# Cosformer attention and a token mixer on one core: two heads stacked per row tile, single-copy q, column tiles, 256 KB stores and a written-out order

## The chip, the cores and the metric

The kernel runs on one core of one Trainium2 chip. The metric is the device time of that core in microseconds (us), as the median of several executions. The profile comes from one execution and counts from the first to the last instruction; that is its span.

A core has five engines that each work through a queue of their own in order: PE (TensorE, matmuls, with weight loads listed as PEld), DVE (VectorE), ACT (ScalarE), POOL (GpSimd) and SP (SyncE, which here only issues DMAs). They wait for each other by semaphores. TensorE writes to PSUM, from which VectorE and ScalarE read.

## What is computed

B = 8, 8 heads, S = 576 tokens, D = 64 per head, all inputs and the output in fp32.

```python
# attention, per batch and head
r_q, r_k = relu(q), relu(k)                       # 576 x 64
q_p = concat([r_q * cos, r_q * sin], -1)          # cos, sin of pi/2 * position / 576
k_p = concat([r_k * cos, r_k * sin], -1)          # 576 x 128
kv  = k_p.T @ v                                   # 128 x 64
z   = k_p.sum(0)
x   = (q_p @ kv) / (q_p @ z + 1e-6)               # 576 x 64; heads side by side: 576 x 512
# token mixer, per batch
wq, wk = x @ w_q, x @ w_k                         # 576 x 64
mixed  = (wq @ wk.T / 8) @ x                      # as wq @ (wk.T @ x): 64 x 512 between
out    = relu(mixed) @ w_out                      # 576 x 512
```

## The kernel before

The input of one pair of heads lies in HBM as 128 partitions (two heads by 64 rows) by 9 x 64 numbers: partition p of a head holds the nine consecutive tokens 9p to 9p + 8, called chunks c below. H counts blocks of two such pairs (four heads), 16 in all; g counts pairs, 32 in all; b counts batches, and a batch has two blocks. All matmuls are in bf16.

For one block, `load` (L73) brings k, q and v in three DMAs of 576 KB (the first block's in halves). ScalarE makes relu of k (`relu_k`, L164). POOL makes relu of q, written twice side by side (`dup_q`, L197: 2304 numbers a partition), and casts v (`cast_v`, L184). VectorE multiplies k by cos and sin (`mul_k`, L173: 2304 numbers).

For one pair, `qk_pe` (L201) issues 18 matmuls of K'V (L209: 64 rows, 128 features, 65 columns: v and a column of ones for z) and 18 transposes of q (L216), all into one PSUM tile `qk_ps`. VectorE copies K'V out (L221) and multiplies the transposed q by cos and sin (L223; the upper 64 partitions hold cos, the lower ones sin). `num` (L228) issues, for each of two heads, five matmuls of 128 rows and one that adds the 1e-6 (L236, L239). VectorE takes the reciprocal of the denominators (L241) and multiplies (L242); the result is x, in bf16.

The mixer follows one batch behind: `xT` transposes x (L252; ten 128x128 transposes for a block); `wk_stage` (L268, 20 matmuls), `wq_stage` (L282, eight of 288 columns; w_q stands twice so that both row halves hold the result), `kx_stage` (L293, five of 512 columns), `mx` (L309, four steps of two 64-row matmuls), and `wout` (L327), four matmuls of 512 columns for each row tile of 128 tokens, 36 row tiles in all. Each of these results goes through one of two PSUM buffers of two banks (`m2_tile`, L63), and nearly all are copied out by ScalarE (`copy`, L260; relu of mixed, L316). In the last stages VectorE takes some (L262, L318). Tokens stay in the order of the chunks, so a row tile is stored by two DMAs of 64 rows, 128 KB each, whose rows lie nine tokens apart in the output (L341).

Every engine runs its instructions in the order in which the program text issues them. That order is set by the loop over g (L368 to L406) and a tail written out behind it (L408 to L422). SP's queue holds loads and stores in one line: `load(H + 3)` stands at the head of block H's loop body, the stores where `wout` is called. Fourteen warm-up matmuls (L92) and the constants come first.

Of the kernel before, what the change touches and what calls it, by code (L numbers as in the profile page):

```python
# [15 lines left out]
I32 = mybir.dt.int32  # L17
AF = mybir.ActivationFunctionType
ALU = mybir.AluOpType
FMAX = 3.4028234e38  # L20
EPS_HI = 9.9837780e-07


@with_exitstack
def kernel(
# [15 lines left out]
    P = 128  # L41
    NPAIR = NH // 2
    C9 = (2 * S) // P
    NDM = DM // P
    SC = S // P + 1
    scale_moe = 1.0 / math.sqrt(DH)

    NB = 2 * B
    HC = C9 * D
    SLOTS = C9 + 1  # L50

    consts = ctx.enter_context(tc.tile_pool(name="consts", bufs=1))
    inp = ctx.enter_context(tc.tile_pool(name="inp", bufs=4))
    prep = ctx.enter_context(tc.tile_pool(name="prep", bufs=2))
    small = ctx.enter_context(tc.tile_pool(name="small", bufs=3))
    xpool = ctx.enter_context(tc.tile_pool(name="xpool", bufs=3))
    moe = ctx.enter_context(tc.tile_pool(name="moe", bufs=2))
    mixpool = ctx.enter_context(tc.tile_pool(name="mixpool", bufs=2))
    outpool = ctx.enter_context(tc.tile_pool(name="outpool", bufs=3))
    psum = ctx.enter_context(tc.tile_pool(name="psum", bufs=1, space=bass.MemoryType.PSUM))  # L60
    ctx.enter_context(tc.manual_schedule())

    def m2_tile(dtype, name):  # L63
        return psum.tile([P, 2, 512 if dtype is FP32 else 1024], dtype,
                         name=name, tag="m2", bufs=2)

    srcs = {}
    for nm, src in (("k", k), ("q", q), ("v", v)):
        srcs[nm] = [src[b].flatten().rearrange("(pr p e) -> p pr e", pr=NPAIR, p=P)
                    for b in range(B)]  # L70
    raw = {}

    def load(H, nsplit=1, names=("k", "q", "v")):  # L73
        b, h0 = divmod(2 * H, NPAIR)
        step = 2 // nsplit
        for nm in names:
            raw[nm, H] = inp.tile([P, 2, HC], FP32, name=f"{nm}f")
        for sp in range(nsplit):
            for nm in names:
                lo = sp * step  # L80
                nc.sync.dma_start(raw[nm, H][:, lo:lo + step, :],
                                  srcs[nm][b][:, h0 + lo:h0 + lo + step, :])

    load(0, nsplit=2)

    warm = consts.tile([P, 512], BF16)
    nc.vector.memset(warm, 1.0)
    warm_ps = m2_tile(FP32, "warm_ps")

    def warm_up(n):  # L90
        for _ in range(n):
            nc.tensor.matmul(warm_ps[:, 0, :], warm[:, 0:P], warm,  # L92
                             start=True, stop=True)

    warm_up(14)

    wq_f = consts.tile([P, NDM, DH], FP32)
    wk_f = consts.tile([P, NDM, DH], FP32)
    wo_f = consts.tile([P, NDM, DM], FP32)

    coef = math.pi / 2.0 / S
    ki = consts.tile([P, C9, 2], I32)
    qi = consts.tile([P, C9, D], I32)
    for hh in range(2):
        ph = slice(64 * hh, 64 * hh + 64)
        nc.gpsimd.iota(ki[ph, :, 0], pattern=[[-1, C9]], base=S, channel_multiplier=-C9)
        nc.gpsimd.iota(ki[ph, :, 1], pattern=[[1, C9]], base=0, channel_multiplier=C9)
    nc.gpsimd.iota(qi[0:64], pattern=[[-1, C9], [-C9, D]], base=S, channel_multiplier=0)
    nc.gpsimd.iota(qi[64:128], pattern=[[1, C9], [C9, D]], base=0, channel_multiplier=0)
    cossin = consts.tile([P, C9, 2, D], BF16)  # L110
    cst = consts.tile([P, C9, D], BF16)
    nc.scalar.activation(cossin, ki.unsqueeze(3).to_broadcast([P, C9, 2, D]),
                         AF.Sin, bias=0.0, scale=coef)
    nc.scalar.activation(cst, qi, AF.Sin, bias=0.0, scale=coef)

    ident = consts.tile([P, P], BF16)
    make_identity(nc, ident)

    ones_t = consts.tile([P, P], BF16)
    nc.gpsimd.memset(ones_t, 1.0)  # L120
    eps_t = consts.tile([P, SC], BF16)
    nc.gpsimd.memset(eps_t, 0.0)
    nc.gpsimd.memset(eps_t[0:1, :], EPS_HI)
    nc.gpsimd.memset(eps_t[32:33, :], 1.0e-6 - EPS_HI)

    v_bufs, qpt_bufs, xT_bufs = [], [], []
    for i in range(3):
        vb = consts.tile([P, 2, C9, D + 2], BF16, name=f"v_buf{i}")
        nc.gpsimd.memset(vb[:, :, :, D:D + 2], 1.0)
        v_bufs.append(vb)  # L130
    for i in range(3):
        qb = consts.tile([P, 2, SLOTS, D], BF16, name=f"qpt_buf{i}")
        nc.gpsimd.memset(qb[:, :, 0, :], 0.0)
        qpt_bufs.append(qb)
    for i in range(2):
        xb = consts.tile([P, NDM, SLOTS * D], BF16, name=f"xT_buf{i}")
        nc.gpsimd.memset(xb[:, :, 0:D], 0.0)
        xT_bufs.append(xb)

    wqq_sb = consts.tile([P, NDM, 2, DH], BF16)  # L140
    wk_sb = consts.tile([P, NDM, DH], BF16)
    wo_sb = consts.tile([P, NDM, DM], BF16)

    def load_w():
        nc.sync.dma_start(wq_f, moe_w_q.rearrange("(c p) j -> p c j", p=P))
        nc.sync.dma_start(wk_f, moe_w_k.rearrange("(c p) j -> p c j", p=P))
        nc.sync.dma_start(wo_f, moe_w_out.rearrange("(c p) n -> p c n", p=P))

    def cast_w(part):
        if part == 0:  # L150
            nc.scalar.copy(wqq_sb, wq_f.unsqueeze(2).to_broadcast([P, NDM, 2, DH]))
            nc.scalar.copy(wk_sb, wk_f)
        else:
            nc.scalar.copy(wo_sb[:, 2 * part - 2:2 * part, :],
                           wo_f[:, 2 * part - 2:2 * part, :])

    kp, qd, rks = {}, {}, {}

    def relu_k(H, lo, hi, eng):
        if lo == 0:  # L160
            rks[H] = prep.tile([P, 2, C9, D], BF16, name="rk")
        o = rks[H][:, lo:hi].rearrange("p r c d -> p r (c d)")
        if eng is nc.scalar:
            nc.scalar.activation(o, raw["k", H][:, lo:hi, :], AF.Relu)  # L164
        else:
            eng.tensor_scalar(o, raw["k", H][:, lo:hi, :], FMAX, 0.0,
                              op0=ALU.min, op1=ALU.max)

    def mul_k(H, lo, hi):
        if lo == 0:  # L170
            kp[H] = prep.tile([P, 2, C9, 2, D], BF16, name="kp")
        n = hi - lo
        nc.vector.tensor_mul(  # L173
            kp[H][:, lo:hi],
            rks[H][:, lo:hi].unsqueeze(3).to_broadcast([P, n, C9, 2, D]),
            cossin.unsqueeze(1).to_broadcast([P, n, C9, 2, D]))

    def cast_v(H, lo, hi, eng):
        src = raw["v", H][:, lo:hi, :].rearrange("p r (c d) -> p r c d", c=C9)
        dst = v_bufs[H % 3][:, lo:hi, :, 0:D]  # L180
        if eng is nc.scalar:
            nc.scalar.copy(dst, src)
        else:
            eng.tensor_scalar(dst, src, 1.0, 1.0, op0=ALU.mult, op1=ALU.mult)  # L184

    def dup_q(H, lo, hi, eng):
        if lo == 0:
            qd[H] = prep.tile([P, 2, C9, 2, D], BF16, name="qd")
        n = hi - lo
        dst = qd[H][:, lo:hi].rearrange("p r c w d -> p (r c) w d")  # L190
        src = raw["q", H][:, lo:hi, :].rearrange(
            "p r (c d) -> p (r c) d", c=C9).unsqueeze(2).to_broadcast(
                [P, n * C9, 2, D])
        if eng is nc.scalar:
            nc.scalar.activation(dst, src, AF.Relu)
        else:
            eng.tensor_scalar(dst, src, FMAX, 0.0, op0=ALU.min, op1=ALU.max)  # L197

    xs, kvs, xTs, wkjs, wqTs, kxs, mixs = {}, {}, {}, {}, {}, {}, {}

    def qk_pe(g):  # L201
        H, i = divmod(g, 2)
        qk_ps = psum.tile([P, 2, 2048], mybir.dt.uint8, name="qk_ps", bufs=1)
        qt = qk_ps[:, :, 0:2 * HC].bitcast(BF16)
        kvp = qk_ps[:, :, 2 * HC:2 * HC + 4 * (D + 1)].bitcast(FP32)
        for c in range(C9):
            for hh in range(2):
                p0 = hh * 64
                nc.tensor.matmul(  # L209
                    kvp[:, hh, :], kp[H][p0:p0 + 64, i, c, :, :],  # L210
                    v_bufs[H % 3][p0:p0 + 64, i, c, 0:D + 1],
                    start=(c == 0), stop=(c == C9 - 1))
        for c in range(C9):
            for hh in range(2):
                p0 = hh * 64
                nc.tensor.transpose(  # L216
                    qt[:, hh, c * D:(c + 1) * D],
                    qd[H][p0:p0 + 64, i, c, :, :],
                    ident[p0:p0 + 64, p0:p0 + 64])
# [148 lines left out]
    for g in range(NG):  # L368
# [12 lines left out]
        if g >= 1:  # L381
            num(g - 1)
# [70 lines left out]
```

## Time and profile before

| | us |
|---|---|
| median of 3 runs | 152.29 |
| lowest and highest run | 151.88, 154.79 |
| span of the profiled execution | 149.6 |
| median less that span | 2.7 |
| TensorE busy, of the span | 115.7 |
| VectorE busy | 90.6 |
| ScalarE busy | 88.1 |
| POOL busy | 56.8 |

The execution that was profiled has no time of its own beside its span; the 2.7 us is the distance to the median. The DMAs moved 39.07 MB for the kernel (29.62 MB read, 9.44 MB written, by the page's own account of HBM). The mean granted clock of TensorE is 0.93 of full speed.

To read the page: matmuls overlap, and each record has a pipeline's length of about 0.19 us on it, so the cost of a matmul in a stream is the distance between starts, not its duration. A group's line ends with the idle time of the engine before those instructions and what ended it. In the answer by windows a row has the stretch, its length, the busy time of PE, PEld, DVE, ACT and POOL with counts, the granted clock, the DMA engines' busy share (slightly over 1 is possible) and GB/s.

### The profile page before, as it was taken

What the parts mean: (1) busy time and instruction counts of PE and PEld (TensorE: products, weight loads), DVE (VectorE), ACT (ScalarE), POOL (GpSimd) and SP (SyncE); (2) the same over time, 40 slices, a digit from 0 to 9 for tenths busy, and PEclk for the clock granted to TensorE, in tenths of its full rate; (3) what the DMA queues carried; (4) which work ended last, traced back from release to release, by engine and by line L of the source; (5) the groups of instructions that cost most, each with busy time, mean ns of one, the idle gap of its engine ahead of it and who ended that gap; (6) DMA issues with size and microseconds to landing.
All of it is one profiled execution on the core that took longest, in us unless ns stands there. A gap on an engine that the chain in (4) does not pass through costs nothing. (4 is left out here: it accounts for less than half of the span.)

```text
span 149.6 us, 4978 instructions
## 1 busy us (share of the span) xinstructions
PE 115.7 (77%) x2155; PEld 77.5 (52%) x2182; DVE 90.6 (61%) x156; ACT 88.1 (59%) x114; POOL 56.8 (38%) x56
## 2 busy tenths in 40 slices
PE   6924663969889988998898987888989896894910
PEld 2214553856567657654765665557656664461400
DVE  1278363979777685947596957375959563325110
ACT  8230076467977787668768757687784566243220
POOL 7638248683561808160817164408170000000000
PEclk9985576589999999999999999999999999999996
DMA  5999999999988999996999998999921811566195
GB/s 163 307 397 338 390 391 391 391 390 390 391 279 182 332 302 323 328 379 148 296 326 343 318 400 278 314 296 307 329 81 42 184 31 24 116 143 142 24 203 124
DMA packets 20469, 39.38 MB, mean 263 GB/s; under 512 B 3040, under 2 KB 3040, under 8 KB 20448
## 3 DMA queue, kind: packets, MB, share of 16 engines
q1 hardware_dynamic: 20448, 39.07, 81.2%
q8 instruction: 17, 0.28, 0.7%
q14 instruction: 4, 0.03, 0.1%
HBM read 29.62 MB, written 9.44 MB: 261 GB/s over the span
## 5 line engine op out<-in xcount | busy, mean ns | idle before, releaser
L197 POOL TENSOR_SCALAR qd<-qf 128x2304 bf16<-128x2304 f32 (+1 forms) x17 | 35.6, 2092 | 52.1 <-PE qk_ps L216 30.6
L327 PE MATMUL o_ps<-wo_sb,mix_sb 128*128 128x512 bf16 x124 | 33.6, 379 | 3.6 <-ACT mix_sb L316 1.8
L164 ACT ACTIVATE rk<-kf 128x1152 bf16<-128x1152 f32 (+1 forms) x17 | 18.9, 1111 | 18.4 <-DMA kf<-in_k_dram 9.2
L260 ACT COPY o_sb<-o_ps 128x512 f32<-128x512 f32 (+1 forms) x24 | 18.4, 765 | 17.9 <-PE o_ps L327 8.3
L242 DVE TENSOR_TENSOR x_sb<-num_ps,rec 128x640 bf16<-128x640 f32 x32 | 26.4, 825 | 1.1
L221 DVE CAST kv_sb<-qk_ps 128x130 bf16<-128x130 f32 x32 | 9.4, 293 | 26.7 <-PE qk_ps L216 26.4
L209 PE MATMUL qk_ps<-v_buf,kp 64*128 64x65 bf16 x576 | 15.8, 199 | 11.0 <-POOL v_buf L184 7.2
L223 DVE TENSOR_TENSOR qpt_buf<-qk_ps,cst 128x1152 bf16<-128x1152 bf16 x32 | 23.9, 748 | 0.0
L173 DVE TENSOR_TENSOR kp<-rk,cossin 128x2304 bf16<-128x2304 bf16 (+1 forms) x17 | 22.2, 1305 | 1.6 <-ACT rk L164 1.6
L327 PEld LDWEIGHTS <-mix_sb 128*128 128x128 bf16 x144 | 13.3, 97 | 15.2 <-issue 3.1
L209 PEld LDWEIGHTS <-kp 64*128 64x128 bf16 x576 | 11.9, 99 | 17.2 <-issue 8.7
L316 ACT ACTIVATE mix_sb<-mx_ps 128x576 bf16<-128x576 f32 x29 | 17.5, 655 | 4.7 <-PE mx_ps L309 4.7
L260 ACT COPY xT_buf<-xT_ps 128x1152 bf16<-128x1152 bf16 x15 | 16.8, 1119 | 4.8 <-PE xT_ps L252 4.8
L184 POOL TENSOR_SCALAR v_buf<-vf 128x1152 bf16<-128x1152 f32 x15 | 17.3, 1151 | 1.2
L236 PE MATMUL num_ps<-kv_sb,qpt_buf 128*128 128x65 bf16 x320 | 17.4, 202 | 0.0
L236 PEld LDWEIGHTS <-qpt_buf 128*128 128x128 bf16 x320 | 13.4, 102 | 3.6 <-issue 1.7
L216 PE MATMUL qk_ps<-ident,qd 64*128 64x64 bf16 x576 | 14.8, 197 | 0.0
L309 PE MATMUL mx_ps<-wqT,kx 64*128 64x288 bf16 x64 | 8.0, 285 | 7.0 <-ACT xT_buf L260 3.9
L252 PE MATMUL xT_ps<-ident,x_sb 128*128 128x128 bf16 x160 | 12.2, 227 | 0.2 <-ACT mix_sb L316 0.2
L216 PEld LDWEIGHTS <-qd 64*128 64x128 bf16 x576 | 11.8, 100 | 0.0
L252 PEld LDWEIGHTS <-x_sb 128*128 128x128 bf16 x160 | 10.4, 102 | 1.9 <-issue 0.2
L239 PE MATMUL num_ps<-eps_t,ones_t 128*128 128x5 bf16 x64 | 11.2, 174 | 0.0
(44 smaller groups left out, 97.9 us busy)
## 6 DMA issues: line engine op xcount, KB each, us to landing
out_dram<-o_sb SPq DMA_DIRECT2D x72, 128.0 KB, 3.3
kf<-in_k_dram SPq DMA_DIRECT2D x15, 576.0 KB, 6.7
qf<-in_q_dram SPq DMA_DIRECT2D x15, 576.0 KB, 7.7
vf<-in_v_dram SPq DMA_DIRECT2D x15, 576.0 KB, 8.5
wo_f<-in_moe_w_out_dram SPq DMA_DIRECT2D x1, 1024.0 KB, 9.9
kf<-in_k_dram SPq DMA_DIRECT2D x2, 288.0 KB, 4.0
qf<-in_q_dram SPq DMA_DIRECT2D x2, 288.0 KB, 4.3
vf<-in_v_dram SPq DMA_DIRECT2D x2, 288.0 KB, 5.3
```

The source lines that it names most:

```text
L164: nc.scalar.activation(o, raw["k", H][:, lo:hi, :], AF.Relu)
L173: nc.vector.tensor_mul(kp[H][:, lo:hi], rks[H][:, lo:hi].unsqueeze(3).to_broadcast([P, n, C9, 2, D]), cossin.unsqueeze(1).to_broadcast([P, ...
L197: eng.tensor_scalar(dst, src, FMAX, 0.0, op0=ALU.min, op1=ALU.max)
L209: nc.tensor.matmul(kvp[:, hh, :], kp[H][p0:p0 + 64, i, c, :, :], v_bufs[H % 3][p0:p0 + 64, i, c, 0:D + 1], start=(c == 0), stop=(c == C9 - 1))
L216: nc.tensor.transpose(qt[:, hh, c * D:(c + 1) * D], qd[H][p0:p0 + 64, i, c, :, :], ident[p0:p0 + 64, p0:p0 + 64])
L223: nc.vector.tensor_mul(qpt_bufs[g % 3][:, :, 1:SLOTS, :], qt.rearrange("f h (c d) -> f h c d", c=C9), cst.unsqueeze(1).to_broadcast([P, 2, ...
L236: nc.tensor.matmul(nv[:, hh, u, :], qpt_bufs[g % 3][:, hh, 2 * u:2 * u + 2, :], kvs[g][:, hh, :], start=(u == 0), stop=False)
L242: nc.vector.tensor_tensor(xs[b][:, :, 2 * pr:2 * pr + 2, :].rearrange("p u h d -> p h u d"), nv[:, :, :, 0:D], rec.to_broadcast([P, 2, SC, ...
L252: nc.tensor.transpose(xT_ps[:, i, u * P:(u + 1) * P], xs[b][:, u, 2 * hp:2 * hp + 2, :], ident)
L260: nc.scalar.copy(dst, src)
L316: nc.scalar.activation(dst, mx_ps[:, :, 0:hs], AF.Relu, scale=scale_moe)
L327: nc.tensor.matmul(o_ps[:, r, :], mixs[bp][:, dmc, rt * P:(rt + 1) * P], wo_sb[:, dmc, :], start=(dmc == 0), stop=(dmc == NDM - 1))
```

## The change

The whole body is rewritten. What it does, part by part:

- **K'V.** cos and sin are multiplied into v and no longer into k. VectorE's product (VS) writes v cos and v sin side by side with two more columns each that hold cos and sin themselves, so that z comes out of the same matmul. The stationary operand is relu of k, 64 rows by 64 columns, and the moving one has 130 columns. The four combinations of head pair and row half are four 64x64 tiles of the array, 36 matmuls for a block.
- **q.** POOL writes relu of q once, two heads of different pairs side by side, so a transpose gives 128 features of two heads: 18 transposes for a block. VectorE (QM) writes q cos and q sin of a block in one product of 2304 numbers from PSUM.
- **num.** cos and sin parts are separate matmuls of 64 rows that add up in PSUM: 20 and two small ones for a pair (N).
- **x transposes.** 20 of 64 rows and 64 columns in place of ten of 128 (XT); the copy takes 1280 numbers a partition.
- **wq.** w_q stands once; eight matmuls of 128 rows write to partitions 0 to 63 and 64 to 127 in turn, for two halves of the tokens (WQ). The copy (288 numbers, before 576) puts tokens into their natural order.
- **Stores.** Because of that order a row tile is 128 consecutive rows of the output: one store of 256 KB, 36 in all, from eight buffers.
- **Engines.** relu of k goes from ScalarE to POOL; all of v's casts are on POOL; the weights are cast in six pieces.
- **PSUM.** One two-bank tile for K'V and transposed q (PQ), one for num (PN), two for all else (PM0 and PM1), the latter given out bank by bank where one bank is enough. k, q and v in fp32 have four buffers, their bf16 forms two.
- **Order.** The warm-up matmuls are gone. A text names every step with its number, its bank and its engine, and a loop issues them in that order.

The first and last lines of the order, and the core of the new functions (L stands for a load, ST for a store, E or a swapped name for a copy out of PSUM):

```python
ORDER = """
LV0 LK0 TB0 CV0@G LQ0 LV1 RK0@G VS0@V LK1 RQ0@G KV0 QT0 KE0@V CV1@G RK1@G QM0@V LV2 LQ1 VS1@V N0
...
KX1:11 X9@V KV6 LK8 XT4:0 XK1:11@A XE4:0@A QT6 N10 VS7@V LK9 LQ8 WO2:11 MX6:0 OE2:11@A ME6:0@A
...
ME30:1@A ST26 ST22 WO29:01 ST27 MX28:1 ME28:1@A WO30:00 OE29:01@V WO34:11 WO35:10 ST29 OE30:00@A
ST30 OE34:11@A ST28 ST34 WO33:00 WO32:01 OE35:10@A ST35 OE33:00@A ST33 OE32:01@V WO31:10
OE31:10@A ST32 ST31
"""
...
    def RQ(H, ps, eng):
        relu(eng, rq_b[H % NPREP].rearrange("p c r d -> p r c d"),
             raw["q"][H % NRAW].rearrange("p r (c d) -> p r c d", d=D))
...
    def VS(H, ps, eng):
        V.tensor_mul(
            v2_b[H % NV2][:, :, :, :, 0:D],
            vb_b[H % NPREP].unsqueeze(3).to_broadcast([P, 2, C, 2, D]),
            vtab.unsqueeze(1).to_broadcast([P, 2, C, 2, D]))
...
    def KV(H, ps, eng):
        for c in range(C):
            for pr, r in ((0, 0), (1, 1), (1, 0), (0, 1)):
                a = slice(H2 * r, H2 * r + H2)
                o = slice(H2 * pr, H2 * pr + H2)
                nc.tensor.matmul(
                    kv_v[o, r, :], rk_b[H % NPREP][a, pr, c, :],
                    v2_b[H % NV2][a, pr, c, :, 0:D + 1],
                    start=(c == 0), stop=(c == C - 1))

    def QT(H, ps, eng):
        for c in range(C):
            for r in range(2):
                a = slice(H2 * r, H2 * r + H2)
                nc.tensor.transpose(qt_v[:, r, c * H2:(c + 1) * H2],
                                    rq_b[H % NPREP][a, c, :, :], ident[a, a])

    def KE(H, ps, eng):
        cast(eng, kv_b[H % 2][:, :, :, 0:D + 1],
             kv_v.rearrange("p r (s e) -> p r s e", s=2))

    def QM(H, ps, eng):
        V.tensor_mul(
            qm_b[H % NQM][:, :, :, 0:C, :].rearrange("p s r c d -> p s r (c d)"),
            qt_v.unsqueeze(1).to_broadcast([P, 2, 2, S]),
            qtab.rearrange("p s c d -> p s (c d)").unsqueeze(2).to_broadcast([P, 2, 2, S]))
...
    def N(g, ps, eng):
        H, r = divmod(g, 2)
        for u in range(SC):
            for s in range(2):
                for pr in range(2):
                    a = slice(H2 * pr, H2 * pr + H2)
                    nc.tensor.matmul(
                        nv[:, pr, u, :], qm_b[H % NQM][a, s, r, 2 * u:2 * u + 2, :],
                        kv_b[H % 2][a, r, s, 0:D + 1],
                        start=(u == 0 and s == 0), stop=False)
...
    def XT(H, ps, eng):
...
        for u in range(SC):
            for w in range(2):
                for t in range(2):
                    a = slice(H2 * t, H2 * t + H2)
                    hd = 4 * h + 2 * w
                    nc.tensor.transpose(o[:, t, w, u, :], x_b[b % NX][a, u, hd:hd + 2, :],
                                        ident[a, a])
...
    def WQ(b, ps, eng):
        o = bank(ps)
        for m in range(NDM):
            for t in range(2):
                nc.tensor.matmul(
                    o[H2 * t:H2 * t + H2, 0:HS], wqw[:, m, :],
                    xT_b[b % NXT][:, m, 0:C, 32 * t:32 * t + 32],
                    start=(m == 0), stop=(m == NDM - 1))

    def QW(b, ps, eng):
        cast(eng, wq_b[b % 2].rearrange("p (i c) -> p i c", c=C),
             bank(ps)[:, 0:HS].rearrange("p (c i) -> p i c", c=C))
...
    out_t = out.flatten().rearrange("(t p e) -> t p e", t=NT, p=P)

    def ST(i, ps, eng):
        nc.sync.dma_start(out_t[i], o_b[i % NOUT])
```

The other steps keep their form: RK and CV are the relu of k and the cast of v, X the reciprocal and the product of num, XE the copy of transposed x, WK and KX with their copies KW and XK, MX and its relu ME, WO and its copy OE. In the text a step's number counts blocks (KV, QT, VS, XT), pairs (N, X), batches (WK, WQ, KX), or single tiles (MX, WO).

## The prediction

> **What bounds the kernel now.** I read the page first (busy shares, the slices), then cut the span into three stages at starts of K'V products (L209) and asked for the engines' busy time in each, then the timeline of TensorE inside the steady stage, then the groups of VectorE. The page:
>
> ```profile
> span 149.6 us, 4978 instructions
> ...
> PE 115.7 (77%) x2155; PEld 77.5 (52%) x2182; DVE 90.6 (61%) x156; ACT 88.1 (59%) x114; POOL 56.8 (38%) x56
> ...
> PEclk9985576589999999999999999999999999999996
> DMA  5999999999988999996999998999921811566195
> GB/s 163 307 397 338 390 391 391 391 390 390 391 279 182 332 302 323 328 379 148 296 326 343 318 400 278 314 296 307 329 81 42 184 31 24 116 143 142 24 203 124
> ```
>
> No engine is full, and the DMA runs at its 390 GB/s only in the first 40 us. The stages say more. The first K'V starts at 8.03, that of the fifth block of four heads (g = 8) at 37.67, that of the last block (g = 30) at 117.61:
>
> ```profile
> 8.03:37.67 29.64, 17.98 (x438) 15.38 (x439) 20.81 (x36) 13.76 (x16) 17.46 (x10) 0.71 1.06 385
> 37.67:117.61 79.94, 71.42 (x1476) 48.37 (x1497) 57.01 (x100) 58.49 (x76) 34.22 (x22) 1.00 0.87 282
> 117.61:149.60 31.99, 20.49 (x233) 11.76 (x234) 10.87 (x18) 11.57 (x17) 0.00 (x0) 0.96 0.49 107
> ```
>
> (Length, busy PE, PEld, DVE, ACT, POOL, clock, DMA share, GB/s.) The first stage is the DMA's, 385 GB/s, and TensorE's clock is 0.71 there. The middle, 11 blocks in 79.9 us, is TensorE's: 71.4 busy, 89%; VectorE and ScalarE have 57 and 58. The tail is again TensorE's chain, and then the stores. How TensorE streams:
>
> ```profile
> 60.92 1.14 PE L282 MATMUL wq_ps<-xT_buf,wqq_sb 128*128 128x288 bf16 x8
> 62.00 0.46 PE L209 MATMUL qk_ps<-v_buf,kp 64*128 64x65 bf16 x18
> 62.29 0.42 PE L216 MATMUL qk_ps<-ident,qd 64*128 64x64 bf16 x18
> 62.79 0.42 PE L309 MATMUL mx_ps<-wqT,kx 64*128 64x288 bf16 x4
> 63.15 0.33 PE L236 MATMUL num_ps<-kv_sb,qpt_buf 128*128 128x65 bf16 x5
> 63.31 0.17 PE L239 MATMUL num_ps<-eps_t,ones_t 128*128 128x5 bf16 x1
> 63.34 0.32 PE L236 MATMUL num_ps<-kv_sb,qpt_buf 128*128 128x65 bf16 x5
> ...
> 65.55 0.72 PE L252 MATMUL xT_ps<-ident,x_sb 128*128 128x128 bf16 x10
> ```
>
> A matmul of 288 columns costs (1.14 - 0.29)/7 = 0.122 us, 0.42 ns a column, in a stream. Eighteen of 65 columns with 64 rows take 62.00 to 62.29 = 0.29, 0.016 each and not 0.027: the two row halves run at once. wq ends streaming at 60.92 + 8 x 0.122 = 61.90 and L209 starts at 62.00, so a change of tile shape costs 0.10.
>
> **Working, against the profiled span.** The span is 149.6; the median of the runs is 152.3, 2.7 more, which I add at the end.
>
> TensorE's unit prices now: K'V 0.29 and q transposes 0.24 a pair of heads; num 0.37 (12 in 63.15 to 63.52); x transposes 10 x (0.72 - 0.23)/9 = 0.55; wq 0.98; mx 0.13 a step (two pairs in 0.42 - 0.285); wk (20 in 0.75) 0.58; kx (5 of 512 columns in 1.24) 1.08; wout 4 x 0.216 = 0.86 a row tile. For the middle as it is: 22 pairs x 0.90 = 19.8, 12 xT 6.6, 5.5 batches x 2.64 = 14.5, 22 mx 2.9, 24 row tiles 20.6, some 46 shape changes 4.6; together 69 of 79.9, a density of 0.87. That is what this style of in-order streams with two PSUM buffers reached.
>
> Changed TensorE prices, per block of four heads. K'V: 36 matmuls of 64x64 with 130 columns, each 0.055. If four quadrants run at once, 9 x 0.055 = 0.50; two at once, 0.99 (now 0.58); one at a time, 1.98. No row shows column tiles; nearest are the row halves, which do overlap fully, so I take 0.50. q transposes: 18 in place of 36, 0.24 less 0.24 saved. num: 22 of 64 rows in pairs, 11 slots of 0.031 = 0.34, if row halves pair as in L209; 0.68 if not. x transposes: 20 of 64 columns in pairs, 0.27 (was 0.55). wq in column pairs: 0.49 (0.98 if they do not pair). The rest is unchanged. Shape changes: 66 before, 107 in the fixed order (12 up to the fifth K'V, 64 up to the last, 29 after).
>
> [...]
>
> VectorE, by its groups kept apart by shape:
>
> ```profile
> L242 DVE TENSOR_TENSOR x_sb<-num_ps,rec 128x640 bf16<-128x640 f32 x32 | 26.4, 825 | 1.1
> L223 DVE TENSOR_TENSOR qpt_buf<-qk_ps,cst 128x1152 bf16<-128x1152 bf16 x32 | 23.9, 748 | 0.0
> L173 DVE TENSOR_TENSOR kp<-rk,cossin 128x2304 bf16<-128x2304 bf16 x15 | 20.7, 1379 | 1.6 <-ACT rk L164 1.6
> L221 DVE CAST kv_sb<-qk_ps 128x130 bf16<-128x130 f32 x32 | 9.4, 293 | 26.7 <-PE qk_ps L216 26.4
> ```
>
> Per block: VS, 2304 elements, as L173 (1379 ns; 0.547 ns an element between its two forms); QM 2304 from PSUM: L223 gives 748 at 1152 like L173's 749, so 1.38; KE 260 elements, 293 + 130 x 1.03 = 0.43 (1.03 is the step from kx 692 to wkj 824); X twice, 2 x (0.215 + 0.825). Sum 5.27, against 5.54 now. If VS (rows of 66) or QM (an operand repeated over two halves) fell to the 1.03 ns of those copies, each would cost 1.15 more; both are 16-bit with unit steps as L173 and L223 are, so I take 1.38.
>
> ScalarE loses relu of k (18.9); its xT copy grows from 1152 to 1280 elements, 1.12 to 1.23; wq's copy halves. POOL loses half of dup_q (2.2 to 1.15) and gains relu of k: 48 x 1.15 = 55, as now. Both stay below VectorE, so I cost them at nothing; were ScalarE's copies late, TensorE's banks would be late next. The warm-up (14 matmuls) goes; the clock before was at 0.5 from 10 us on in spite of it, so 0, at most 3 us in the first stage.
>
> *First stage.* The loads are V, K, Q in that order, the weights spread. V4 and K4 are the last of 8.5 MB, which by the GB/s row land at 25. VectorE, from about 6.5 (a 576 KB load, then a 1.15 cast; its first product now is at 7.2), has 5 VS, 4 KE and QM, 6 X: 6.9 + 7.2 + 6.2 = 20.3, at 0.87 23.4. Fifth K'V at 30 (now 37.7): 7.7 won.
>
> *Middle, 11 blocks.* TensorE: K'V 5.5, q 2.7, num 21 x 0.34 = 7.1, xT 3.0, wk 2.9, kx 5.4, wq 2.5, 20 mx 2.6, 18 row tiles 15.5, 64 changes 6.4: 53.6. VectorE: 11 x (1.38 + 0.43 + 1.38) + 21 x 1.04 + one wq copy 0.5 = 57.4. ScalarE 47. DMA: 31 loads and 13 stores, 21.7 MB at 390 GB/s = 55.6. So VectorE becomes the bound, with DMA and TensorE just below. At density 0.87: 66 (now 79.9). Last K'V at 96.
>
> *Tail.* The fixed order leaves 18 of 36 row tiles behind the last K'V, where before had 11: 15.5 + 12 mx 1.6 + N 1.4 + xT 0.8 + wk, kx, wq 4.3 + K'V and q 0.7 + 29 changes 2.9 = 27.2. These are mostly independent, so density 0.9: 30.2. Then a last copy 0.6 and the store. Now the last copy ends at 143.15 but SP issues ten 128 KB stores at 0.6 each until 146.8 and the end is 149.6; one 256 KB store should need an issue between 0.41 (loads) and 0.6, then the same 2.75: 3.2, against 6.4. Tail 34, against 32.
>
> Sum: 30 + 66 + 34 = 130, plus 2.7: 132.7. SP's queue is in order too: a store waiting for its copy holds the loads behind it. Now, by SP's own timeline, it issued the seventh block's loads up to 33.0 and then stood before the first store until 42.5; in the new order only 13 stores stand ahead of the last loads, so I charge nothing more.
>
> **Rivals.**
> 1. *Column tiles run two at a time.* TensorE's middle is 53.6 + 5.5 + 2.5 = 61.6, at 0.87 70.8, 4.8 more, and the tail 1.6 more: 139. For: no row here shows column tiles. Against: row halves overlap to 3 ns. 0.13. (One at a time adds 16.3 + 2.5 in the middle: 83.2 there, 30 + 83 + 37 + 2.7 = 152, no change; within the cases below.)
> 2. *The order is tight.* Chosen by hand or by a planner, it may reach 0.97: first stage 28, middle 59, tail 28 + 3.6: 121. For: PSUM in four single banks. Against: PQ and PN have one buffer each. 0.15.
> 3. *In-order waits.* VectorE reaches only the 0.71 (57.0 of 79.9) it has now: 57.4/0.71 = 81, 15 more: 147. Place: QM needs the transposes, these need POOL's RQ, which needs the previous block's buffers (two each). 0.12.
> 4. *Slower: VectorE loses its rate in VS and QM.* Middle (57.4 + 25.3)/0.87 = 95, first stage 40: 172. With VS alone it is 80 + 35 + 34 + 2.7 = 152, so it decides when both go. For: outputs in rows of 66, a repeated PSUM operand. Against: L173 and L223 have repeated operands at 0.55 to 0.65 ns. 0.07.
> 5. *No change*: num and K'V unpaired, or VS alone, 150 to 154: 0.05.
>
> **How the numbers follow.** My forecast (124 to 139 by itself) has 0.48. About 2% is what a measurement of this kernel tells from no change: 149.2 to 155.3. Faster: the forecast, rivals 1, 2 and most of 3, 0.48 + 0.13 + 0.15 + 0.11 = 0.87; within: 0.05 + 0.01 = 0.06; slower 0.07. The range leaves out rival 4, the best of rival 2 and the end of 5: 121 to 150. Predicted: the forecast, 132.7.
>
> **What would show it.** Right: fifth K'V at 30, last at about 96; in the middle VectorE at 85% or more; K'V of a block 0.50; VS and QM at 1.38; the last copy 3 us before the end. Wrong: K'V at 1 us or more (rival 1); VS or QM above 2 us (rival 4); VectorE waiting in long pieces on POOL or PE (rival 3). A first stage still at 37, with the DMA at its limit, would break the first term; a tail with TensorE under 0.8 the last.

## The result and the profile after

The changed kernel takes 147.77 us (median of 4 runs, 147.21 to 148.23) against 152.26 for the kernel before in the same session: a ratio of 0.9741, 95% interval 0.9684 to 0.9797. It is faster, by 2.6%, where 12.9% had been forecast: the direction is right and the size is wrong. The page of the profiled execution, line by line as shown of before (span, busy time, clock, DMA):

```profile
span 146.4 us, 5267 instructions
...
PE 104.8 (72%) x2341; PEld 65.7 (45%) x2360; DVE 92.8 (63%) x128; ACT 68.5 (47%) x106; POOL 65.7 (45%) x68
...
PEclk9999999999779969999999999999999999998797
```

TensorE is busy for 11 us less and ScalarE for 20 us less, yet the span is only 3.2 us shorter, and TensorE's share has gone from 77% to 72%: more of the time is waiting. The three stages, cut at the same places (first, fifth and last K'V, now L222; columns as in the prediction):

```profile
8.35:31.33 22.98, 15.23 (x442) 12.61 (x443) 19.23 (x25) 5.33 (x8) 15.94 (x13) 1.00 1.06 383
31.33:103.96 72.63, 59.77 (x1548) 38.51 (x1555) 55.68 (x76) 42.91 (x66) 42.93 (x34) 0.95 0.87 316
103.96:146.40 42.44, 29.81 (x361) 14.56 (x364) 16.08 (x26) 16.17 (x27) 0.00 (x0) 0.94 0.33 125
```

| | before | forecast | after | off by |
|---|---|---|---|---|
| fifth K'V starts at | 37.67 | 30 | 31.33 | 1.3 |
| middle | 79.94 | 66 | 72.63 | 6.6 |
| tail | 31.99 | 34 | 42.44 | 8.4 |

So two terms failed, the tail first. In the tail TensorE is at 29.8 of 42.4. The waits of that stretch (who waited for whom; us in total, times, longest):

```profile
DVE o L194 <- PE ps_m L351: 6.9, 3, 3.9
...
ACT o L190 <- DVE o L194: 6.4, 2, 4.7
...
DVE o L194 <- ACT o L190: 5.1, 2, 3.4
```

The last two are odd. Two copies of finished row tiles, of different banks into different buffers, only read PSUM: why should one wait for the other? The timeline shows it at work:

```profile
119.19 0.58 ACT L190 COPY o<-ps_m 128x512 f32<-128x512 f32 x1 [1.38 <-PE ps_m L351]
...
119.81 0.69 DVE L194 COPY o<-ps_m 128x512 f32<-128x512 f32 x1 [1.70 <-ACT o L190]
...
120.55 1.02 PE L351 MATMUL ps_m<-wow,mix 128*128 128x512 bf16 x3 [1.04 <-DVE o L194]
```

The order's words there are `WO20:01 WO25:00 ... OE25:00@A X31@V OE20:01@V`: ScalarE copies bank 0 of PM0 and VectorE bank 1. VectorE, idle for 1.70, starts 0.04 us after ScalarE ends, and TensorE starts 0.05 us after VectorE ends. Both banks are one declared tile, `[P, 2, 2048]`. That suggests that the waits are made by declared tile: copies by two engines out of one tile stand in line, and a copy of one bank waits for matmuls issued before it into the other. The first experiment tries it.

The middle shows something else. TensorE's own records stop and go on with no release in between ("issue" in brackets), in the midst of a K'V:

```profile
38.95 0.76 PE L222 MATMUL ps_qk<-v,rk 64*64 64x130 bf16 x19 [0.93 <-issue]
...
52.15 0.40 PE L222 MATMUL ps_qk<-v,rk 64*64 64x130 bf16 x8 [1.36 <-issue]
...
64.81 0.81 PE L351 MATMUL ps_m<-wow,mix 128*128 128x512 bf16 x3 [1.12 <-issue]
```

Seven such pauses above 0.15 us in this stage add up to 5.4 us; the kernel before has none. The same stretch has two dents of the clock row: it is at 0.50 from 38.6 to 42.0 and from 52.2 to 55.6. A third, from 134.2 to 137.6, lies in the tail.

### The profile page after: what moved, and what is told of

It is laid out like the page before. It is cut to its first block, busy times and chain, and to the rows that moved or that the text cites. A ratio compares the mean times of both kernels' runs of the same rounds, so it can differ in the third digit from the quotient of the medians.

```text
span 146.4 us, 5267 instructions
## 1 busy us (share of the span) xinstructions
PE 104.8 (72%) x2341; PEld 65.7 (45%) x2360; DVE 92.8 (63%) x128; ACT 68.5 (47%) x106; POOL 65.7 (45%) x68
## 5 line engine op out<-in xcount | busy, mean ns | idle before, releaser
L351 PE MATMUL ps_m<-wow,mix 128*128 128x512 bf16 x130 | 36.4, 396 | 9.1 <-ACT o L190 3.0
L186 POOL TENSOR_SCALAR rq<-qraw 128x1152 bf16<-128x1152 f32 x16 | 22.3, 1395 | 16.2 <-DMA qraw<-in_q_dram 7.6
L209 DVE TENSOR_TENSOR v<-vb,vtab 128x2304 bf16<-128x2304 bf16 x16 | 24.7, 1542 | 4.7 <-POOL vb L192 4.5
L266 DVE TENSOR_TENSOR x<-ps_num,rec 128x640 bf16<-128x640 f32 x32 | 26.4, 825 | 1.1
L186 POOL TENSOR_SCALAR rk<-kraw 128x1152 bf16<-128x1152 f32 x16 | 21.2, 1323 | 8.1 <-DMA kraw<-in_k_dram 2.6
L343 ACT ACTIVATE mix<-ps_m 128x576 bf16<-128x576 f32 x31 | 19.5, 655 | 11.2 <-PE ps_m L332 11.2
L222 PE MATMUL ps_qk<-v,rk 64*64 64x130 bf16 x576 | 14.4, 246 | 14.1 <-POOL rk L186 9.9
L192 POOL TENSOR_SCALAR vb<-vraw 128x1152 bf16<-128x1152 f32 x16 | 19.0, 1190 | 8.7 <-DMA vraw<-in_v_dram 8.1
L190 ACT COPY xT<-ps_m 128x1280 bf16<-128x1280 bf16 x14 | 17.1, 1229 | 9.9 <-PE ps_m L283 9.7
L239 DVE TENSOR_TENSOR qm<-ps_qk,qtab 128x2304 bf16<-128x2304 bf16 x16 | 21.6, 1347 | 0.0
L252 PE MATMUL ps_num<-kvs,qm 64*128 64x65 bf16 x640 | 17.1, 200 | 4.1 <-DVE qm L239 3.5
L222 PEld LDWEIGHTS <-rk 64*64 64x64 bf16 x576 | 10.8, 122 | 15.6 <-POOL rk L186 10.1
L265 DVE RECIPROCAL rec<-ps_num 128x10 f32<-128x10 f32 x32 | 6.9, 216 | 11.2 <-PE ps_num L258 10.9
## 6 DMA issues: line engine op xcount, KB each, us to landing
vraw<-in_v_dram SPq DMA_DIRECT2D x16, 576.0 KB, 11.1
kraw<-in_k_dram SPq DMA_DIRECT2D x16, 576.0 KB, 10.9
wqf<-in_moe_w_q_dram SPq DMA_DIRECT2D x1, 128.0 KB, 11.1
```

Of the source, the lines that this page charges most:

```text
L186: eng.tensor_scalar(dst, s, FMAX, 0.0, op0=ALU.min, op1=ALU.max)
L190: A.copy(dst, s)
L192: G.tensor_scalar(dst, s, 1.0, 1.0, op0=ALU.mult, op1=ALU.mult)
L209: V.tensor_mul(v2_b[H % NV2][:, :, :, :, 0:D], vb_b[H % NPREP].unsqueeze(3).to_broadcast([P, 2, C, 2, D]), vtab.unsqueeze(1).to_broadcast( ...
L222: nc.tensor.matmul(kv_v[o, r, :], rk_b[H % NPREP][a, pr, c, :], v2_b[H % NV2][a, pr, c, :, 0:D + 1], start=(c == 0), stop=(c == C - 1))
L239: V.tensor_mul(qm_b[H % NQM][:, :, :, 0:C, :].rearrange("p s r c d -> p s r (c d)"), qt_v.unsqueeze(1).to_broadcast([P, 2, 2, S]), qtab.re ...
```

## The experiments

Theory A says that the tail is lost to waits by declared tile. Theory S says that the middle is lost where TensorE's instructions come too slowly. The other letters are rivals. Ratios are to the kernel before, in shared runs.

**Four one-bank tiles.** MX's two halves then need two copies of 288 columns, and XE two of 640. The order stays.

```diff
-    PM = [psum.tile([P, 2, 2048], U8, name=f"ps_m{i}") for i in range(2)]
+    PM = [[psum.tile([P, 2048], U8, name=f"ps_m{i}{j}") for j in range(2)] for i in range(2)]
```

> The changed kernel with the two two-bank PSUM tiles of the mixer (PM0, PM1) declared as four one-bank tiles, the order text untouched; the relu of mixed and the copy of transposed x become two instructions of one bank each. That adds some 7 us to ScalarE's 68.5 (31 relus from one of 655 ns to two of about 0.41, 14 copies from 1.23 to two of about 0.70). Theory A: the tail (42.4 us against 34 forecast) and part of the middle are long because the waits go by declared tile, so that a copy of one bank waits for matmuls or copies of the other; then the tail falls to 35 to 37 and the span from 146.4 to about 137 (134 to 141). Theory B: the tail is the order's own serial chain of the last batch; then the tail stays at 41 or more and the span at 145 to 148. Theory C (POOL beside VectorE slows both): no change either, 145 to 148.

137.33 us, ratio 0.903 (0.8954 to 0.9106). By stages (the last two; fifth K'V at 33.29):

```profile
33.29:104.38 71.09, 60.59 (x1548) 38.07 (x1554) 56.83 (x76) 44.88 (x96) 41.43 (x33) 0.95 0.87 314
104.38:135.77 31.39, 27.46 (x360) 13.31 (x364) 16.53 (x29) 17.41 (x41) 0.00 (x0) 1.00 0.44 169
```

The tail falls from 42.4 to 31.4, more than the 35 to 37 expected, though ScalarE and VectorE have 17 more instructions in it; the middle moves by 1.5. The last row tiles now run through, and a copy waits for nothing but its own matmuls:

```profile
127.71 4.48 PE L353 MATMUL ps_m<-wow,mix 128*128 128x512 bf16 x20
127.91 0.59 ACT L190 COPY o<-ps_m 128x512 f32<-128x512 f32 x1 [0.26 <-PE ps_m L353]
```

Theory A is borne out, and the rivals set beside it for the tail are not. (The split of MX's and XE's copies came with the declaration and was not tried alone; by estimate up to 1.7 of the 11 us, half of 3.4 us at clock 0.50, is the dent that this tail does not have.) The pauses stay (7.7 us).

**Relu of k back on ScalarE.** In the changed kernel, `RK0@G` to `RK15@G` became `@A`.

> The changed kernel with relu of k back on ScalarE (16 instructions of about 1.17 us there), in the same places of the order. Theory C: POOL's three casts a block run beside VectorE's products and each slows the other (VS 1542 ns where 1379 was measured before, relu of q 1395 and relu of k 1323 where 1151 was priced); then VS falls to about 1.4, the middle by 3 to 6 us and the span to about 141 to 143. Theories A and B: the middle does not hang on POOL; ScalarE gets 19 us more and stands before k's loads in its queue, so the span stays or grows, 146 to 152.

152.11 us, ratio 1.0064 (1.0017 to 1.011): 4.3 us slower than the changed kernel. POOL does slow VectorE's VS: it falls from 1542 ns to 1350, near the 1379 of the product of that size in the kernel before. But the time goes elsewhere:

```profile
L209 DVE TENSOR_TENSOR v<-vb,vtab 128x2304 bf16<-128x2304 bf16 x16 | 21.6, 1350 | 4.7 <-POOL vb L192 4.6
...
L184 ACT ACTIVATE rk<-kraw 128x1152 bf16<-128x1152 f32 x16 | 18.6, 1165 | 14.1 <-DMA kraw<-in_k_dram 14.1
```

ScalarE now stands 14.1 us before k's loads, and copies that TensorE needs stand behind it. The price of VS was real. Since the move brought waits of its own, this run does not show what a faster VS alone would be worth.

**The store part alone.** The kernel before with wq's columns in token order and one store per row tile:

```diff
-                    xT_bufs[b % 2][:, dmc, D + nh * hs:D + (nh + 1) * hs],
+                    xT_bufs[b % 2][:, dmc, D:].rearrange("p (c i) -> p c i", c=C9)[
+                        :, :, 32 * nh:32 * nh + 32],
...
-        copy(eng, wqT, wq_ps[:, :, 0:hs])
+        copy(eng, wqT.rearrange("p h (i c) -> p h i c", c=C9),
+             wq_ps[:, :, 0:hs].rearrange("p h (c i) -> p h i c", c=C9))
...
-                nc.sync.dma_start(dst, o_sb[hi * 64:hi * 64 + 64, r, :])
+            nc.sync.dma_start(
+                out.flatten().rearrange("(t p e) -> t p e", p=P, e=DM)[bp * C9 + rt0 + r],
+                o_sb[:, r, :])
```

> The kernel before with one part of the change alone: wq takes its columns in token order and its copy permutes them, so that a row tile is one store of 256 KB. Forecast's last term: from the last copy to the end 3.2 us in place of 6.4, and less time of SP before the loads; 148 to 150 where before has 152.3 (ratio 0.975 to 0.985). If the ten queued stores at the end were not what set the end: 152 or more, since ScalarE's permuted copy costs the same or more.

147.76 us, ratio 0.973 (0.9664 to 0.9795), a gain of 4.0 us by itself: as much as the whole change gave. From the last copy to the end it takes 3.6 us, where the kernel before took 6.4: the last term of the forecast had the direction and nearly the size (3.2).

**Fewer loads.** The four-bank kernel without `LQ4` to `LQ15`. It leaves out the loads of q from the fifth block on, and POOL reads old q in their place.

> The kernel with four one-bank tiles, without the loads of q from the fifth block on (POOL then reads old q, so the output is not the reference's): 7.1 MB less of 39. It asks about TensorE's pauses in which it waits for nothing (0.8 to 1.9 us each, 6.9 us in all, 255 or a multiple of 255 weight loads and matmuls apart; 18 transfers of 16 KB on the instruction queue). Theory D: an instruction block arrives late because the data transfers hold it up; then the pauses shrink to 2 us or less in all, as the DMA is no longer full from 33 us on. Theory E: the block is asked for too late for bursts of 40 to 110 short instructions, whatever the DMA does; then 5 us or more remain. If they are no instruction fetches at all, they need not stand 255 apart. The span also loses what the loads of q held up: 130 to 134 by either.

131.4 us in one run, against 137.33. The pauses fall from 7.7 to 2.0 us, and the middle from 71.1 to 64.2 with the DMA at 0.69. Fewer bytes do thin the pauses, to the edge of what theory D expected, which speaks for a supply that competes with the loads. It is not proof: without these loads TensorE's other waits change as well.

**Transposes of x as before.** The four-bank kernel with ten 128x128 transposes in place of twenty 64x64 per block, and plain copies: 320 fewer TensorE instructions (a matmul and a weight load count as two), but 16 x 0.28 = 4.5 us more streaming by the prediction's prices.

```diff
-                for t in range(2):
-                    nc.tensor.transpose(o[t][:, w, u, :], x_b[b % NX][a, u, hd:hd + 2, :], ident[a, a])
+                nc.tensor.transpose(o[:, 2 * u:2 * u + 2, :], x_b[b % NX][:, u, hd:hd + 2, :], ident)
```

> The kernel with four one-bank tiles and one part of the change undone: x is transposed by ten matmuls of 128x128 a block as before (0.55 us) and not by twenty of 64 rows (0.27), and the two copies write plain runs. TensorE streams 16 x 0.28 = 4.5 us more, and 320 of 4700 instructions go, 1.25 blocks of 256. If TensorE's streaming is the limit: 2 to 4 us slower than 137.3. If TensorE's instruction supply is: the same or 1 to 2 us faster. Forecast's price of this part (0.27 in place of 0.55) says slower.

133.59 us, ratio 0.8878 (0.881 to 0.8945): 3.7 us faster than the four banks alone by the medians, 2.3 by the ratios, with more streaming. It is the fastest version of this study that loads everything. Its stages:

```profile
8.46:32.04 23.58, 16.06 (x425) 13.01 (x425) 18.07 (x25) 5.36 (x10) 17.74 (x13) 1.00 1.06 383
32.04:100.20 68.16, 61.73 (x1449) 39.41 (x1444) 56.99 (x76) 45.18 (x96) 42.52 (x34) 1.00 0.91 332
100.20:132.01 31.81, 28.24 (x334) 14.13 (x333) 16.47 (x29) 17.21 (x40) 0.00 (x0) 1.00 0.44 166
```

The pauses are 4.7 us, and the clock does not fall in these stages; with four banks alone it was at 0.50 from 38.2 to 45.0. Two other readings of the gain drop out. The plain copies are no cheaper (701 ns each, 698 with four banks alone). And TensorE changes its tile shape more often, not less: 118 times in the whole kernel, where the changed kernel and the four-bank one have 107.

**Half stores.** The four-bank kernel with two stores of 64 rows per row tile.

> The kernel with four one-bank tiles and one part undone: each row tile is stored by two DMAs of 64 rows and 128 KB (72 in all). SP issues 36 more at 0.4 to 0.6 us. If the issue sets the tail, as before, the distance from the last copy to the end grows from 3.3 to about 4 to 6 and the time by 2 to 4 us, to 139 to 141; if the new order spreads the stores well enough, less than 1 us.

142.15 us, ratio 0.9411 (0.9305 to 0.9516): 4.8 us more by the medians, 5.8 by the ratios. (Its profiled execution lay above its median, at 143.74.) From the last copy to the end it takes 8.5 us in place of 2.9, more than the 4 to 6 expected. SP's queue is the end of it:

```profile
119.71 19.40 SPq L364 DMA_DIRECT2D out_dram<-o  x29
```

29 stores take 19.4 us; from 122.6 on they stand back to back, one each 0.65 us. The four-bank tail needs the large stores.

**Two raw buffers.** Four banks and the old transposes, with two raw buffers each of k, q and v in place of four (`NRAW` 4 to 2).

> The kernel with four banks and 128x128 transposes (133.6 us), with two buffers in place of four for each of the raw q, k and v blocks: at most six 576 KB loads can then stand issued and not landed, where now one takes 11 us to land at 1.5 us each, so some seven stand ahead of whatever comes after them. Theory S (the 16 KB fetches of TensorE's instructions stand behind the issued loads): the fetches, 6.1 to 6.2 us apart from 31 to 87 us now, come closer together wherever TensorE wants it, the pauses with nothing waited for fall from 4.7 us to under 2, and the time to 130-132 if the loads still keep the DMA engines full. Rival S2 (it is the full DMA engines that make a fetch slow, however few loads stand issued): spacing 6.1 to 6.2 and 4 to 5 us of pauses stay, 133-135. Rival S3 (the pauses do not come from the fetches at all): they stay at their counts whatever the spacing. In all three, if two buffers starve the loads, the GB/s row shows holes before 90 us and the time is 135-140; the pauses are then read by themselves.

148.59 us, ratio 0.9804 (0.973 to 0.9877). The order's text issues ten loads ahead of the conversion of the block that they replace, so parts of eight blocks are computed from later data; the work is the same. (The profiled execution lay above the median, at 150.49.) The loads were starved:

```profile
GB/s 142 402 395 394 364 386 56 110 309 401 393 390 361 297 328 256 22 380 359 379 338 403 385 352 314 182 239 306 103 311 111 4 141 4 141 216 82 275 342 218
```

So the time tells nothing of the fetches, as the expectation allowed. Loads landed in 6.9 us instead of 11. From 34 to 46 us, where the row above has 361 to 401 GB/s, the fetches stood 6.3 and 5.9 us apart, as S2 had it; later they were 3.5 to 10.9 apart. The pauses that follow a fetch fell to 1.0 us, under the 2 of theory S, but TensorE stood for data so often that fetches had time to come. This decides nothing between S and S2.

**More matmuls.** Four banks and the old transposes, and 12 tiny 64x64 matmuls behind each K'V (`for _ in range(3)` over the four tiles, two columns each).

> The kernel with four banks and 128x128 transposes (133.6 us), with twelve more 64x64 matmuls of two columns and their twelve weight loads behind each K'V, into unused bytes of the same banks, read by nobody: 384 more TensorE instructions, that is 1.5 fetches of 256. Theory S (TensorE gets no more than 256 instructions per 6.2 us while the loads last): about twelve of the sixteen blocks lie in that stretch, so +1.5 x 6.2 x 12/16 = +7 us, 140-141, with more or longer pauses. Rival streaming (36 such pairs of K'V stream in 0.50 us, so twelve take 0.17, 16 of them 2.7 us): 136 or less, pauses as before. Rival no effect (they fit beside other work): 133-134.

139.06 us, ratio 0.9189 (0.9136 to 0.9242): some 5 us more than without them (5.5 by the medians, 4.7 by the ratios), between S's +7 and streaming's 2.7. The pauses grew from 4.7 to 7.3 us, and with the 2.7 of streaming that makes 5.3; but the clock, too, fell to 0.50 from 38.6 to 42.0. A cost beyond streaming is there, smaller than S had it, and the clock may have a part in it.

**The changed kernel with the old transposes.** Two-bank tiles kept.

> The changed kernel with its two-bank tiles kept and only the transposes of x undone (ten 128x128 in place of twenty 64x64 per block, one plain copy): 320 TensorE instructions fewer. Theory S with waits by tile as a separate cost: the gain is the one seen with four banks, 3.7 us, so 144, ratio 0.975 to the changed kernel and 0.948 to the kernel before; pauses fall below 5 us. Rival (the waits by tile cover the fetches: TensorE stands anyway while they come): under 1.5 us, 146.5-148. Rival (streaming decides, 10 x 128x128 cost 0.28 us more per block than 20 x 64x64): slower, 149-152.

144.96 us, ratio 0.9563 (0.9491 to 0.9635), 2.7 us less than the changed kernel by the ratios. Pauses 2.5 us in place of 5.4. The stages separate the two causes:

```profile
32.00:101.51 69.51, 60.21 (x1437) 39.76 (x1444) 57.30 (x76) 43.05 (x66) 43.36 (x34) 1.00 0.91 326
101.51:144.00 42.49, 30.56 (x331) 15.29 (x334) 16.01 (x25) 16.17 (x27) 0.00 (x0) 0.94 0.33 125
```

The middle falls by 3.1 and the tail stays at 42.5. With four banks the tail fell by 11.1 and the middle by 1.5. Two separate losses, in two stages. The middle's goes with the short transposes; by which path, the next part argues.

**What the pauses are.** The page of the four-bank kernel lists, beside the kernel's own DMAs, a queue that carries instructions:

```profile
q1 hardware_dynamic: 19824, 39.07, 79.1%
q8 instruction: 18, 0.29, 0.9%
```

They are 18 packets of 16,384 bytes. TensorE's instruction counts at the pauses lie 255 or 256, or a multiple, apart, so I take a packet to hold 256, an estimate from these counts. Five of these packets in the four-bank kernel, from the trace:

```
packet starts   TensorE stops   goes on   after the packet's start   instruction
51.31           52.51           53.81     2.50                       1726
57.59           59.22           60.00     2.42                       1981
63.70           64.29           66.20     2.50                       2236
69.88           70.96           72.39     2.52                       2491
80.25           81.14           82.59     2.34                       3001
```

From 30 us on, at all pauses above 0.3 us but one (0.35, with two raw buffers), TensorE goes on 2.2 to 2.7 us after a packet's start. (Those of 0.22 us at 55.03 in the changed kernel and at 44.26 in the four-bank one, which the sums hold, stand behind no packet.) While the loads fill the DMA engines (busy share 1.04 to 1.06 up to 69 us in the four-bank kernel) the packets come no closer than about 6 us in most of the stretch (6.28, 6.11, 6.18 here). In the kernel with fewer loads they come 3.3 to 5.5 us apart from 61 us to the tail, but for one of 6.5. So I read a pause as what is left of the 2.4 us when TensorE has used up its instructions. The kernel before has 17 such packets, mostly 4 to 8 us apart, and no pause: it has 4337 of these records against 4701, and longer ones. That its pace alone spares it is argued, not shown.

## Why the prediction was wrong, point by point

**First stage: right.** 30 forecast, 31.33 measured, at 383 GB/s, with VectorE at 84% where the sum took 0.87. The clock was 1.00 there without the warm-up matmuls.

**Middle: too short by 6.6.** The prices of the parts held, but for VS:

| | forecast | measured |
|---|---|---|
| K'V, 36 matmuls in four tiles | 0.50 | 0.72 record, 0.50 from the first start to the last |
| QM | 1.38 | 1.347 |
| KE | 0.43 | 0.428 |
| VS | 1.38 | 1.542 |
| xT copy | 1.23 | 1.229 |

Column tiles run four at once (0.50 measured, where two at once were priced at 0.99), so rival 1 is out; VS and QM stayed far under the 2 us of rival 4, so that is out. The changes of tile shape cost what the sum gave them: 66 in the middle (64 forecast), and 0.31 us in the median from the start of a 512-column matmul to the next shape, 0.216 of it streaming, which leaves the 0.10 of the sum. The changes are not what is missing.

What failed is "At density 0.87: 66" (69 of 79.9 is 0.86, which makes it 66.5): VectorE's 57.4 us of work took 72.6, a density of 0.79. The 0.87 was taken from the kernel before, and the change cuts TensorE's work into more and shorter instructions. The middle holds 5.4 us of pauses, which no part of the sum held, and 6.8 us at clock 0.50 (by estimate at most half of that, 3.4, lost). How the 6.6 splits is not settled: both shrank together in the two kernels where the transposes were undone, 3.1 and 2.9 us came back there, and the fastest version has 4.7 us of pauses left in a middle of 68.2, so the pauses cannot simply be added to the 66. Waits by tile have a part too: 69.5 with two-bank tiles, 68.2 without. VS was mis-sized by 0.16 x 11 = 1.8 us of VectorE's time, but with VS at 1600 ns the fastest version still had its middle near the 66. VectorE at 85% or more did not come either: 77% after, 84% in the fastest version.

**Tail: too short by 8.4.** "These are mostly independent, so density 0.9: 30.2" is the step that failed. The work is independent, but its waits are not. The last copy ends at 142.88, so the 27.2 us of work took 38.9, a density of 0.70. With one-bank tiles the tail is 31.4 and the last copy ends at 132.8: 28.4 for the same work, 0.96. Rival 2 spoke for a tight order with "PSUM in four single banks"; the code declares two tiles of two banks, and I read the hand-out of banks as if it were the declaration. The line "were ScalarE's copies late, TensorE's banks would be late next" named the right chain and priced it at nothing. The place was in plain view: the old tail, too, copies both banks of one tile by ScalarE, then VectorE, and VectorE stood 3.3 us in two waits for ScalarE's copies there:

```profile
L262 DVE COPY o_sb<-o_ps 128x512 f32<-128x512 f32 x2 | 1.4, 692 | 3.3 <-ACT o_sb L260 3.3
```

**Last store: right.** 3.2 forecast from the last copy's end, 3.55 measured (142.88 to 146.43). Alone it gave 4.0 us on the kernel before, and undoing it with four banks cost 4.8.

**Rival 3** put a wait in the place of the gain and came nearest in time (147), but by luck: it put all of the loss into the middle, at QM and POOL's buffers, where half of it was in the tail. With two-bank tiles and short transposes both undone the kernel runs in 133.59 us, and stages of 32.0, 68.2 and 31.8 stand against the forecast's 30, 66 and 34. That is not the kernel of the forecast (its transposes are the old ones), and its three errors partly cancel; but it is where the sum comes close.

## What to carry to other kernels

Before a stage is called independent, look at what a wait is attached to: a buffer handed out in parts but declared as one waited as one here, and splitting the declaration gave 10 us. Count TensorE's instructions as well as its streaming time: here 320 fewer of them gained 2.7 us in one kernel and 2.3 to 3.7 in another, though they stream 4.5 us more by the forecast's prices. And take apart what a large change bundles: its store part alone was worth all that the whole gained.

## What the runs showed that was not expected

- TensorE's instructions came by DMA (by the page 17 packets of 16 KB on the instruction queue in the kernel before, 18 in the changed one), by estimate 256 to a packet, and at such boundaries it stood with nothing else to wait for: up to 1.91 us at a time, 7.5 us in the four-bank kernel, none above 0.15 in the kernel before.
- The granted clock fell to 0.50 for stretches of 3.4 us, or twice that, also where no long stand of TensorE lay ahead: in the 7 us before such a dent the longest was 0.45 us in the four-bank kernel (38.2 to 45.0) and 1.36 in the changed kernel (52.2 to 55.6). It did not fall in the middle of the two kernels in which the transposes were undone, though they had pauses of 1.77 and 1.62. What sets it off was not tried by itself.
- POOL's elementwise work beside VectorE's slowed it: the same product of 2304 numbers took 1350 ns with 52 POOL instructions (relu of k on ScalarE) and, with 68, 1542 in the changed kernel, 1591 with four banks and 1600 with the old transposes too. QM, of the same length but from PSUM, stayed at 1347 to 1348 in these four.
- 36 matmuls of 64x64 with 130 columns stream in 0.50 us from the first start to the last, as the forecast priced four tiles of the array at once.
